# Fewer filler products, one step turned on TensorE, more masks on TensorE and another order in a fused attention and rational-MLP kernel

## The chip, the cores and the metric

One core of one Trainium2 chip. The metric is device time in microseconds (us) of one execution. Engines: PE is TensorE's products, PEld its weight loads, DVE VectorE, ACT ScalarE, POOL GpSimd (which issues most loads here), SP SyncE (which issues stores and DMA transposes).

Each run has a state: slow if it is over 1.5% above the fastest of the same kernel. Verdicts use fast runs. A ratio here is the record's, of one kernel's fast runs to the other's fast runs of the same rounds (the plain ratio of their means agrees within 0.2%). It is not quite the ratio of the medians that are quoted, which are taken over all runs. The profiled executions of both kernels were slow ones; where I compare traces I say so.

## The reference

Attention with 4 sink keys and a window of 128, batch 4, 8 heads, 768 positions, head size 64; then an MLP 512 -> 2048 -> 512 whose activation is a rational function:

```python
scores = q @ k.T / sqrt(64); keep = (pos_k < 4) | (0 <= pos_q - pos_k < 128)
x = softmax(where(keep, scores, -1e9)) @ v            # -> 3072 x 512
h = x @ w_in                                          # 3072 x 2048
P = a0 + a1*h + a2*h**2 + a3*h**3
Q = 1 + |b0|*|h| + |b1|*h**2
out = (P / (Q + 1e-6)) @ w_out
```

## The kernel before

The 3072 rows go in 12 steps of 256, three steps to a batch item. A step is attention (scores, exponentials, masks, values, normalizing), turning x, input projection (4 pieces of 16 products), elementwise work on VectorE and ScalarE, output projection (4 pieces of 8 products). All steps are cut into named pieces; one long list, ORDER, says in which order they are emitted, and each engine works through its own pieces in that order. A negative number -n in ORDER emits n filler products. The parts that the change touches:

```python
PE_MASK = (0, 1, 2, 3, 6, 9)      # steps masked by a product added to the scores
NS_PE = 2                         # steps whose k, q, x TensorE turns
...
def spin(n):                      # filler: result is never read
    for _ in range(n):
        nc.tensor.matmul(ps_scores[:, 0, 384:384 + P], lhsT=ident, rhs=ident, start=True, stop=True)

def mask(s, grp):                 # steps not in PE_MASK: VectorE multiplies the exponentials
    ...
    nc.vector.tensor_tensor(out=blocks, in0=blocks, in1=edge..., op=ALU.mult)

def turn_x(s, part):              # TensorE, through PSUM; ScalarE copies it back (place_x)
    ps = ps_hp.tile([P, 2, 512], FP32, tag="ps_h", name="ps_xT") ...
    for i in range(NPB):
        nc.tensor.transpose(ps[:, i, :], x_n[s][:, part, i * P:(i + 1) * P], ident)
def turn_x_tile(s, part):         # DMA transpose
    nc.sync.dma_start_transpose(out=x_part(s, part), in_=x_n[s][:, part, :])
...
            if s < NS_PE:
                piece(("turn_x", s, part), "PE", ...)
                piece(("placed_x", s, part), "ACT", ...)
            else:
                piece(("turn_x", s, part), "SP", ...)
...
    def parts(m):                 # elementwise work of a step in so many parts
        return 4 if m == LAST else 2 if m == 0 else 1
...
    names = list(work)
    for n in ORDER:
        if n < 0:
            spin(-n)
        elif work[names[n]].run:
            work[names[n]].run()
```

The softmax here doesn't subtract the row's maximum and nothing guards it: scores larger than these inputs give would overflow.

## Time and profile before

| | before |
|---|---|
| median (lowest to highest, 4 runs) | 272.69 us (269.80 to 273.32) |
| profiled execution, span (slow state) | 275.9 us |
| PE / DVE / ACT busy | 252.4 / 225.2 / 221.2 us |
| filler products | 372 |
| first input projection, first elementwise work | 33.3 us, 40.4 us |

The lines on which the argument rests stand in the prediction. A line of the stage view is: stretch, its length, busy time and number of instructions on PE, PEld, DVE, ACT, POOL, then granted TensorE clock, DMA share, GB/s. A line of waits is: who waited for what, total us, times, longest. A line of the chain is: start, length, what, how many.

### The profile page before, as it was taken

The page shows a single profiled execution, that of the slowest core. Times are in us where ns is not written, and L with a number is a line of the kernel's source. Part 1 is how long each engine was busy: PE and PEld are TensorE (multiplying, and loading weights), DVE is VectorE, ACT ScalarE, POOL GpSimd, SP SyncE. Part 2 cuts the span into 40 slices and gives each one's busy share as a digit, 9 for nine tenths or more (in the row PEclk, how much of TensorE's full clock was granted, in tenths as well). Part 3 has the DMA queues.
Part 4 walks back from the last instruction along what each step waited for, and adds up shares of the span by engine and source line. Part 5 has one row for each costly group of instructions (what it writes and reads, how often), then busy time and mean ns, then how long its engine had stood idle before and what let it go on. Part 6 is the DMA issues. An engine that isn't in the chain of part 4 may idle for free.

```text
span 275.9 us, 5692 instructions
## 1 busy us (share of the span) xinstructions
PE 252.4 (91%) x2344; PEld 192.4 (70%) x2344; DVE 225.2 (82%) x283; ACT 221.2 (80%) x201; POOL 118.8 (43%) x170
## 2 busy tenths in 40 slices
PE   2978898888599889999999999999999999999994
PEld 2968797777487587787776778777687776655551
DVE  3244318989917978999999999999999999999981
ACT  6084555898259669998989979999998999999870
POOL 8876677598069304083390990698000000000000
PEclk9997999999979999999999999999999999999999
DMA  6999999979999947599699999699901211211022
GB/s 140 192 162 185 117 112 129 137 85 162 118 79 90 124 74 53 130 105 180 80 74 154 124 110 203 45 139 156 122 4 39 77 57 21 76 76 40 26 88 77
DMA packets 113586, 28.72 MB, mean 104 GB/s; under 512 B 104344, under 2 KB 110488, under 8 KB 113560
## 3 DMA queue, kind: packets, MB, share of 16 engines
q0 software_dynamic: 75568, 13.00, 73.6%
q1 hardware_dynamic: 36464, 14.30, 28.8%
q10 hardware_dynamic: 1528, 1.06, 1.3%
q8 instruction: 18, 0.29, 0.5%
q14 instruction: 8, 0.07, 0.1%
HBM read 27.30 MB, written 6.29 MB: 122 GB/s over the span
## 4 chain that ended last, share of the span: by engine, by line
PE 51%; DVE 26%; ACT 12%; issue 6%; DMA 3%; POOL 1%; POOLq 0%
PE ps_out L664 19%; PE ps_h L596 16%; PE ps_s L432 5%; PE ps_o L524 4%; DMA xblk<-x_n 3%; DVE sq L634 3%; ACT lnq L640 3%; ACT e L480 3%; DVE kT L420 3%; DVE g L650 2%; PE ps_s L468 2%; DVE den L617 2%; DVE x_n L548 2%; ACT hb L603 2%; ACT den L645 2%
## 5 line engine op out<-in xcount | busy, mean ns | idle before, releaser
L596 PE MATMUL ps_h<-xblk,w_in_sb 128*128 128x256 bf16 x768 | 91.5, 276 | 2.6 <-DMA xblk<-x_n 2.5
L664 PE MATMUL ps_out<-w_out_sb,g 128*128 128x512 bf16 x368 | 86.3, 379 | 0.6 <-ACT o_t L673 0.3
L596 PEld LDWEIGHTS <-w_in_sb 128*128 128x128 bf16 x768 | 75.2, 99 | 13.5 <-issue 2.2
L238 POOL DMA_DIRECT2D v_bd<-in_v_dram x96 | 66.9, 723 | 37.1 <-PE ps_o L524 22.5
L664 PEld LDWEIGHTS <-g 128*128 128x128 bf16 x384 | 36.8, 98 | 37.2 <-issue 1.0
L603 ACT ACTIVATE hb<-ps_h 128x1024 bf16<-128x1024 f32 x48 | 48.9, 1033 | 12.9 <-PE ps_h L596 12.7
L480 ACT ACTIVATE e<-ps_s 128x768 bf16<-128x768 f32 x48 | 39.1, 816 | 11.9 <-PE ps_s L471 7.9
L640 ACT ACTIVATE lnq<-den,one_eps,qsc 128x4096 f32<-128x4096 bf16 (+2 forms) x16 | 47.2, 2956 | 0.0
L645 ACT ACTIVATE den<-lnq 128x4096 bf16<-128x4096 f32 (+2 forms) x16 | 44.1, 2771 | 0.0
L432 PE MATMUL ps_s<-ident 128*128 128x128 bf16 x372 | 28.1, 233 | 14.5 <-ACT e L480 9.3
L432 PEld LDWEIGHTS <-ident 128*128 128x128 bf16 x372 | 25.6, 106 | 16.7 <-issue 10.4
L230 POOL DMA_DIRECT2D k_bf<-in_k_dram x22 | 20.1, 916 | 35.5 <-DMA kT_flat<-k_bf 35.3
L524 PE MATMUL ps_o<-v_bd,e 128*128 128x130 bf16 x352 | 28.8, 220 | 1.2 <-DVE x_n L548 0.9
L650 DVE TENSOR_TENSOR g<-num,den 128x4096 bf16<-128x4096 bf16 (+2 forms) x16 | 28.0, 1752 | 1.6 <-ACT den L645 1.3
L468 PE MATMUL ps_s<-qT,kT 128*128 128x192 bf16 x192 | 28.1, 248 | 0.1
L621 DVE TENSOR_TENSOR den<-den,sq 128x4096 bf16<-128x4096 bf16 (+2 forms) x16 | 28.0, 1750 | 0.1
L634 DVE TENSOR_TENSOR sq<-sq,hb 128x4096 bf16<-128x4096 bf16 (+2 forms) x16 | 27.9, 1752 | 0.1
L637 DVE TENSOR_TENSOR num<-num,sq 128x4096 bf16<-128x4096 bf16 (+2 forms) x16 | 27.8, 1749 | 0.0
L524 PEld LDWEIGHTS <-e 128*128 128x128 bf16 x352 | 23.7, 97 | 5.2 <-DVE x_n L548 2.6
L610 ACT ACTIVATE sq<-hb 128x2048 bf16<-128x2048 bf16 (+1 forms) x15 | 25.4, 1695 | 0.1
L617 DVE TENSOR_SCALAR den<-hb 128x2048 uint32<-128x2048 uint32 (+2 forms) x16 | 15.9, 992 | 8.7 <-ACT hb L603 8.6
L222 POOL DMA_DIRECT2D q_bf<-in_q_dram x21 | 20.7, 996 | 0.4 <-DMA v_bd<-in_v_dram 0.4
(86 smaller groups left out, 252.4 us busy)
## 6 DMA issues: line engine op xcount, KB each, us to landing
out_dram<-o_t SPq DMA_DIRECT2D x22, 256.0 KB, 2.3
v_bd<-in_v_dram POOLq DMA_DIRECT2D x96, 32.0 KB, 4.6
k_bf<-in_k_dram POOLq DMA_DIRECT2D x22, 128.0 KB, 4.7
q_bf<-in_q_dram POOLq DMA_DIRECT2D x21, 128.0 KB, 5.2
w_in_sb<-in_moe_w_in_dram POOLq DMA_DIRECT2D x4, 512.0 KB, 7.8
w_out_sb<-in_moe_w_out_dram POOLq DMA_DIRECT2D x4, 512.0 KB, 8.1
stage_b<-in_q_dram ACTq DMA_DIRECT2D x2, 384.0 KB, 6.3
stage_a<-in_k_dram SPq DMA_DIRECT2D x2, 256.0 KB, 5.3
```

The source lines that it names most:

```text
L238: nc.gpsimd.dma_start(out=v_bd[s][e * 64:(e + 1) * 64, i, :, e, 0:D], in_=v[b, h, g * TS:(g + 1) * TS, :].rearrange("(j p) d -> p j d", p=64))
L432: nc.tensor.matmul(ps_scores[:, 0, 384:384 + P], lhsT=ident, rhs=ident, start=True, stop=True)
L468: nc.tensor.matmul(w_, lhsT=kT_fix[s % 2][:, i * NHF + n, :], rhs=qT_fix[b % 2][:, i, c:c + 192], start=True, stop=not on_pe)
L480: nc.scalar.activation(out=data.rearrange("p (a n) c -> p a n c", a=2), in_=ps[:, :, 0:384].rearrange("p a (n c) -> p a n c", n=2), func=A ...
L524: nc.tensor.matmul(ps_o[:, u, :], lhsT=l_, rhs=r_.rearrange("p e c -> p (e c)"), start=(m == 0), stop=(m == len(terms) - 1))
L596: nc.tensor.matmul(ps[:, n, :], lhsT=w_in_all[:, c, fc * P:(fc + 1) * P], rhs=xblk[m][:, c, :], start=(c == 0), stop=(c == NDMC - 1))
L603: nc.scalar.activation(out=hb[m][:, j * GW:(j + 1) * GW], in_=ps_h.pop((m, j)).rearrange("p n c -> p (n c)"), func=AF.Copy)
L634: nc.vector.tensor_tensor(out=sq[m][:, c], in0=sq[m][:, c], in1=hb[m][:, c], op=ALU.mult)
L640: nc.scalar.activation(out=lnq_fix[:, c], in_=den[m][:, c], func=AF.Ln, scale=qsc, bias=one_eps)
L645: nc.scalar.activation(out=den[m][:, c], in_=lnq_fix[:, c], func=AF.Exp, scale=-1.0)
L650: nc.vector.tensor_tensor(out=g_of[m][:, c], in0=num[m][:, c], in1=den[m][:, c], op=ALU.mult)
L664: nc.tensor.matmul(ps_out[m, tt], lhsT=g_of[m][:, co:co + P], rhs=w_out_all[:, fc, :], start=(fc == 0), stop=(fc == NFFC - 1))
```

## The change

The intent: drop nearly all fillers; spare step 2 its DMA transposes, on one of which TensorE waits; take masks off VectorE in three more steps; start step 0's elementwise work after a quarter of its projection; and lay everything out in an order made for that.

```diff
-ORDER = [ ... 968 entries, of them 27 fillers with 372 products ... ]
+ORDER = [ ... 954 entries, of them 2 fillers with 14 products ... ]
-    NS_PE = 2
+    NS_PE = 3
+    CUTS0 = (0, 1, 2, 4)
+    Q0_DVE = (2, 3)
-    PE_MASK = (0, 1, 2, 3, 6, 9)
+    PE_MASK = (0, 1, 2, 3, 5, 6, 8, 9, 10)
@@ place_q0: two of the four copies of step 0's q on VectorE
+        if i in Q0_DVE:
+            nc.vector.tensor_copy(out=dst, in_=src)
+        else:
             nc.scalar.activation(out=dst, in_=src, func=AF.Copy)
@@ the parts of a step
-    def parts(m):
-        return 4 if m == LAST else 2 if m == 0 else 1
+    def cuts(m):
+        return (0, 1, 2, 3, 4) if m == LAST else CUTS0 if m == 0 else (0, 4)
... (place_q1 for any batch item; a piece x_free; sizes from cuts)
```

## The prediction

> **What bounds the kernel now.** I read first the page of the whole span, then the chain that ended last in order of time, then the list of waits, then busy time by stage.
>
> The head of the page and its chain, by engine and line:
>
> ```profile
> span 275.9 us, 5692 instructions
> PE 252.4 (91%) x2344; PEld 192.4 (70%) x2344; DVE 225.2 (82%) x283; ACT 221.2 (80%) x201; POOL 118.8 (43%) x170
> PEclk9997999999979999999999999999999999999999
> ...
> PE ps_out L664 19%; PE ps_h L596 16%; PE ps_s L432 5%; PE ps_o L524 4%; DMA xblk<-x_n 3%; DVE sq L634 3%; ACT lnq L640 3%; ACT e L480 3%; DVE kT L420 3%; DVE g L650 2%; PE ps_s L468 2%; DVE den L617 2%; DVE x_n L548 2%; ACT hb L603 2%; ACT den L645 2%
> ```
>
> Three engines are all above 80% busy, and two things on the chain compute nothing: L432, the filler products (the order list asks for 372), with 5%, and one DMA transpose of x with 3%. Pieces of the chain in order of time (start, length, what):
>
> ```profile
> 5.16 9.08 PE ps_s L432 x113
> ...
> 33.31 1.75 PE ps_h L596 x16
> ...
> 40.42 0.83 DVE den L617
> ...
> 60.72 1.39 PE ps_s L432 x22
> ...
> 65.85 9.48 DMA xblk<-x_n
> 75.38 3.51 PE ps_h L596 x16
> ```
>
> TensorE does nothing real until 14 us; its first input projection is at 33.31, VectorE's first elementwise work at 40.42. The transpose of step 2's x takes 9.48 us, and the 16 products after it take 3.51 instead of 1.75 us, because the clock has dropped. The list of waits (total, times, longest) and the busy time by stage (PE, PE weight load, DVE, ACT, POOL):
>
> ```profile
> DVE rec L536 <- PE ps_o L524: 13.3, 9, 6.7
> ...
> PE ps_s L432 <- ACT e L480: 9.3, 9, 1.8
> ...
> DVE den L617 <- ACT hb L603: 8.6, 1, 8.6
> ```
>
> ```profile
> 33.00:42.00 9.00, 9.00 (x96) 8.23 (x95) 1.58 (x2) 5.75 (x7) 7.16 (x11) 1.00 2.09 116
> ...
> 76.00:90.00 14.00, 13.53 (x125) 10.67 (x124) 6.49 (x10) 11.09 (x7) 11.53 (x17) 0.90 1.09 86
> ...
> 105.00:255.00 150.00, 149.51 (x1271) 108.53 (x1270) 146.59 (x145) 142.50 (x115) 52.02 (x67) 1.00 0.86 95
> ```
>
> So VectorE has two holes: 8.6 us before step 0's elementwise work, and some 7.5 us at 76 to 90 (longest wait 6.7), the echo of the late x. Fillers are not free either: they write the scores' PSUM bank, so nine groups stood waiting for an exponential to empty it, and only then ran ahead of the real scores. From 105 to 255 us the three engines are 95 to 100% busy: nothing is wasted there and nothing can be won but by doing less. The loss is all ahead of 105 us, and in the end.
>
> **What the Trainium skill says.** "TensorE: Matmul & The Clock Gate", Part 1, says that the array runs at half clock until it has been busy for some 3.4 us, and falls back after about as long an idle window; a 128-column product is then 107 ns apart instead of 56. The trace agrees: 113 fillers in 9.08 us are 80 ns each, a mixture of both; and 3.51 against 1.75 us above is a factor of two after 2.5 us of idle time. This is what the fillers are for, and what their removal risks. "DMA: Bandwidth & Descriptors", Anatomy of one DMA, gives a fixed cost of about 2.0 us to a DMA; DMA Transpose (X-bar), Alternative transpose paths, names TensorE, with an identity matrix and an output in PSUM, as the other way. Here x_n's transposes land 2.4, 3.7 and 9.5 us after issue (least, median, most), so they pay the fixed cost and a queue; on TensorE four products and an ACT copy take 0.40 + 0.60 us (L571, L580).
>
> **The change, part by part.**
>
> *Fillers: 372 to 14.* Gone from the chain: L432 is 5.3% of 275.9 = 14.6 us, 9.08 of it at the start. Not all comes back, since the inputs have to arrive. In the new order the q load is issued near 3 us behind a clear; with 6.3 us to landing it is there at 9 to 10. ScalarE then has, up to x's first placing, two casts (0.84 each), four spreads (0.38), a clear (1.04), two placings of step 0's q (0.49), two of later q (0.60), five exps (0.82), two sink exps (0.28, 0.39) and one placing of x (0.60): 1.68 + 1.52 + 1.04 + 0.98 + 1.20 + 4.10 + 0.67 + 0.60 = 11.8 us. That would be 21 us without a wait; the waits at both ends (q turn, scores, attention, norm, turn), at a mostly cold clock, I put at 4 to 7.5. First input projection: 25 to 28.5, say 26.5, so 7 us earlier than 33.3.
>
> *Cold clock.* I expect a half clock for much of the first 26 us (in the waits above) and for the first 3.4 us of the projections: +1.7 us.
>
> *Step 2 turned on TensorE.* It removes the 9.48 us and the 1.75 us of cold projection, and adds on the path one turn and one placing, 1.0 us. Off the path: TensorE 8 + 8 + 8 products of 128 columns (1.4 us), ScalarE 4 placings (2.4 us). Six DMA transposes of step 2 also leave a crowded queue.
>
> *Masks of nine steps instead of six on TensorE.* Steps 5, 8, 10: VectorE loses 6 multiplications of 0.687 (4.1 us); TensorE gains 3 x 16 products of 128 columns at 56 ns (2.7 us). All in the stage where both are full, so it moves work from one co-bound to the other.
>
> *Step 0 in three parts.* The first part begins after one quarter of the projection instead of two: by one projection and its copy, some 2 us earlier. Cost: a third set of VectorE instructions (about 1 us of fixed cost) and a square of 0.7 us moved from ScalarE. Two of the four placings of step 0's q (0.49 each) move from ScalarE to VectorE, which is idle then.
>
> *Sums, three ways, in the terms of the profiled span.* Chain: 275.9 - 14.6 (fillers) - 9.5 - 1.75 + 1.0 - 2 + 4 to 5 (cold clock, later input) + 2.7 (masks, if TensorE bounds) = 256. VectorE: it starts elementwise work at 26.5 + about 3.5 (cold projection) + 1.0 (copy) = 31 instead of 40.4; it had 212 us of work from there on and 23.5 idle, tail included; now 212 - 4.1 + 2 = 210 and 23.5 less the 7.5 hole and a little = 15: 31 + 210 + 15 = 256. TensorE: real products are 768 x 0.109 + 384 x 0.216 + 432 x 0.057 + 192 x 0.082 + 96 x 0.056 + about 7.5 for sinks and turns = 220 us, now 224; about 8.5 of them fall ahead of the first projection; 26.5 + 215.5 + 1.7 (cold) + 3.9 (small waits, as now after 90 us) + 3.3 (copy and store at the end) + about 5 idle in the ramp = 256. The three agree because the engines are balanced. The profiled run was a slow one: 275.9 against a timed median of 272.47, a factor of 0.9876. 256 x 0.9876 = 253.
>
> **The rivals.** (a) *The clock.* Without fillers TensorE stays cold not only at the start but in every gap of the ramp: it did 47 us of real work before 90 us (220 less what I count after), which would double: up to 20 us lost, and the time stays near 260 to 270. For it: the factor of two is in the trace. Against: the idle gaps that fillers covered from 33 to 105 us are mostly below 2 us. (b) *Loads.* POOL issues at 0.65 to 0.9 us a piece and is busy for 25 of the first 33 us, DMA slices are at 9 up to 62 us. If everything wants its data 8 us earlier, values, keys or weights may be late: a wait on input weights or values in place of the fillers, time near 258 to 265. Against: only POOL's own instructions wait for DMA in the list, and steps 0 and 1 need no more data than before. (c) *Balance eats the gain.* Step 3's x still goes by DMA, and TensorE has some 4 us of other work between step 3's attention and its projection, less than a slow landing; a wait of 2 to 5 us there could come back: 255 to 258. (d) *The other way*: the new order also closes small waits and the ramp's idle, with 15 us of VectorE idle falling to 8: near 246.
>
> **Range and chances.** Centre 253. Low end (d), 245; high end (b) or part of (a), 262. To lose the 2% (to be above 267) nearly all of the chain's gain must be taken back by the clock or loads, which I give 5%; slower by 2%, 1%.
>
> **What would show it.** Right: first product of L596 at 25 to 29 us; L432 gone from the chain; no DMA xblk wait ahead of step 2, TensorE clock low in slices 1 to 4 and high from slice 5; VectorE's first L617 at 29 to 33 us; the longest wait of L536 below 4 us; 150 us of the middle still at 97% on DVE. Wrong: low clock digits beyond 40 us (a); waits of TensorE for w_in or v DMA, or DVE idle with POOL full (b); a DMA xblk wait above 5 us at step 3 (c); a middle that has become less dense than now, which I do not allow for at all and which would put the time above 260.

## The result, and the profile after

The changed kernel takes **261.68 us** (median of 4, 260.00 to 264.13) against 272.69: ratio 0.9596, 95% interval 0.9491 to 0.9700, so faster. It lies inside the stated range of 245 to 262, but at its upper edge and 8.7 us above the centre.

The page's head and chain of the changed kernel, and its chain in order of time:

```profile
span 262.4 us, 5089 instructions
PE 236.2 (90%) x2037; PEld 176.0 (67%) x2058; DVE 224.1 (85%) x287; ACT 222.4 (85%) x205; POOL 122.1 (47%) x170
PEclk9999999799995999999999999999999999999999
...
PE 57%; DMA 16%; DVE 11%; issue 5%; ACT 4%; POOL 4%; SPq 1%; ACTq 0%; POOLq 0%
```

```profile
42.76 3.97 DMA v_bd<-in_v_dram
46.78 1.00 PE ps_o L530 x10
47.77 3.13 PE ps_h L602 x16
...
72.48 6.12 DMA xblk<-x_n
78.65 6.57 PE ps_h L602 x32
```

Fillers are gone from the chain, and DMA has gone from 3% of it to 16%. That share is time under way, not time waited for. Two new waits of TensorE stand in the ramp, each shorter than its transfer: 3.15 us for the values of step 2 (landing at 46.7 us) and 2.58 us for the DMA transpose of step 3's x. After each one the input projection runs at half clock in this execution, a slow one: 16 products in 3.13 us, 32 in 6.57, against 1.75 per 16. The waits and stages say the same:

```profile
DVE rec L542 <- PE ps_o L530: 9.5, 11, 2.2
...
DVE den L623 <- ACT hb L609: 4.3, 2, 3.9
...
PE ps_o L530 <- DMA v_bd<-in_v_dram: 3.2, 1, 3.2
...
PE ps_h L602 <- DMA xblk<-x_n: 2.8, 2, 2.6
```

```profile
24.00:33.00 9.00, 8.86 (x96) 8.05 (x96) 4.86 (x12) 6.60 (x8) 6.91 (x10) 1.00 1.99 163
...
42.00:52.00 10.00, 6.85 (x63) 5.67 (x62) 5.10 (x10) 6.58 (x7) 9.16 (x13) 0.83 1.27 118
...
76.00:90.00 14.00, 11.37 (x78) 8.42 (x79) 8.21 (x10) 7.47 (x9) 6.72 (x8) 0.76 1.26 117
```

The start is better than predicted: the first products of L602 stand at 23.3 us in the trace (predicted 26.5), VectorE's first L623 at 26.7 (predicted 31), and that first projection runs warm. Then VectorE stands idle for 4.9 us in 42 to 52 and for 5.8 us in 76 to 90, with the clock at 0.83 and 0.76.

So two questions went to the chip. Which part brought the 11 us? And are those two holes the 9 us that are missing to 253?

### The profile page after: what moved, and what is told of

It is laid out like the page before. It is cut to its first block, busy times and chain, and to the rows that moved or that the text cites. A ratio compares the mean times of both kernels' runs of the same rounds, so it can differ in the third digit from the quotient of the medians.

```text
span 262.4 us, 5089 instructions
## 1 busy us (share of the span) xinstructions
PE 236.2 (90%) x2037; PEld 176.0 (67%) x2058; DVE 224.1 (85%) x287; ACT 222.4 (85%) x205; POOL 122.1 (47%) x170
## 4 chain that ended last, share of the span: by engine, by line
PE 57%; DMA 16%; DVE 11%; issue 5%; ACT 4%; POOL 4%; SPq 1%; ACTq 0%; POOLq 0%
PE ps_out L670 22%; PE ps_h L602 22%; PE ps_o L530 7%; DMA v_bd<-in_v_dram 6%; DMA w_out_sb<-in_moe_w_out_dram 3%; PE ps_s L474 3%; DMA xblk<-x_n 2%; DMA q_bf<-in_q_dram 2%; DMA out_dram<-o_t 2%; DVE sq L640 2%; DVE den L627 2%; POOL v_bd L240 2%; ACT lnq L646 1%; DVE x_n L554 1%; PE ps_s L670 1%
## 5 line engine op out<-in xcount | busy, mean ns | idle before, releaser
L602 PE MATMUL ps_h<-xblk,w_in_sb 128*128 128x256 bf16 x768 | 95.3, 280 | 3.0 <-DMA xblk<-x_n 2.8
L670 PE MATMUL ps_out<-w_out_sb,g 128*128 128x512 bf16 x348 | 83.9, 379 | 4.2 <-ACT o_t L679 3.1
L602 PEld LDWEIGHTS <-w_in_sb 128*128 128x128 bf16 x768 | 76.0, 101 | 16.2 <-DMA xblk<-x_n 2.8
L474 PE MATMUL ps_s<-qT,kT 128*128 128x192 bf16 x192 | 30.0, 248 | 1.6 <-ACT e L486 0.9
L232 POOL DMA_DIRECT2D k_bf<-in_k_dram x22 | 22.8, 1037 | 16.9 <-issue 8.4
L530 PEld LDWEIGHTS <-e 128*128 128x128 bf16 x352 | 24.3, 97 | 8.5 <-issue 4.1
L616 ACT ACTIVATE sq<-hb 128x2048 bf16<-128x2048 bf16 (+1 forms) x15 | 24.4, 1626 | 0.1
L477 PE MATMUL ps_s<-nege,ident 128*128 128x128 bf16 x144 | 23.2, 222 | 0.0
L474 PEld LDWEIGHTS <-kT 128*128 128x128 bf16 x192 | 18.5, 98 | 4.0 <-issue 1.0
L623 DVE TENSOR_SCALAR den<-hb 128x2048 uint32<-128x2048 uint32 (+2 forms) x17 | 16.3, 961 | 4.3 <-ACT hb L609 4.3
```

The source lines that it names most:

```text
L474: nc.tensor.matmul(w_, lhsT=kT_fix[s % 2][:, i * NHF + n, :], rhs=qT_fix[b % 2][:, i, c:c + 192], start=True, stop=not on_pe)
L530: nc.tensor.matmul(ps_o[:, u, :], lhsT=l_, rhs=r_.rearrange("p e c -> p (e c)"), start=(m == 0), stop=(m == len(terms) - 1))
L602: nc.tensor.matmul(ps[:, n, :], lhsT=w_in_all[:, c, fc * P:(fc + 1) * P], rhs=xblk[m][:, c, :], start=(c == 0), stop=(c == NDMC - 1))
L670: nc.tensor.matmul(ps_out[m, tt], lhsT=g_of[m][:, co:co + P], rhs=w_out_all[:, fc, :], start=(fc == 0), stop=(fc == NFFC - 1))
```

## The experiments

All twelve kernels gave the right result. Names with b_ start from the kernel before, with a_ from the changed one. My theory 1: fillers and waits lengthen the chain, each gives back about its share, and in the changed kernel the two new holes take part of it again. The rival, theory 2: fillers pay for themselves by the clock, and the new order makes the gain.

| run | median us (lowest to highest, runs) | ratio to before, 95% |
|---|---|---|
| b_nofill | 263.73 (261.93 to 265.61, 4) | 0.971 (0.958 to 0.984) |
| b_nofill_start | 269.34 (268.11 to 270.47, 4) | 0.989 (0.978 to 1.000) |
| b_x2_pe | 270.81 (269.58 to 273.35, 20) | 0.997 (0.994 to 1.000) |
| b_mask9 | 275.24 (272.92 to 282.47, 16) | 1.010 (1.007 to 1.014) |
| b_parts | 265.89 (264.02 to 267.26, 6) | 0.979 (0.973 to 0.984) |
| changed kernel | 261.68 (260.00 to 264.13, 4) | 0.960 (0.949 to 0.970) |
| a_x2_dma | 266.43 (261.74 to 269.80, 4) | none given |
| a_cuts2 | 261.44 (259.63 to 264.49, 6) | 0.962 (0.956 to 0.968) |
| a_mask6 | 274.47 (272.35 to 277.79, 16) | 1.007 (1.003 to 1.010) |
| a_v2_first | 261.52 (258.77 to 266.26, 6) | 0.955 (0.948 to 0.961) |
| a_x3_pe | 259.63 (258.58 to 260.44, 6) | 0.952 (0.948 to 0.957) |
| a_v2_x3 | 257.18 (255.15 to 260.01, 6) | 0.941 (0.934 to 0.948) |
| a_v2_x3_o3 | 256.82 (253.31 to 260.22, 6) | 0.942 (0.934 to 0.950) |

The kernel before, run beside them, had medians of 272.6 to 273.5 us. At the 2% line the record calls the changed kernel, a_v2_first, a_x3_pe and a_v2_x3 faster, b_x2_pe, b_mask9 and a_mask6 the same, and the rest unclear (a_x2_dma has no verdict).

### b_nofill: only the fillers go

```diff
     names = list(work)
-    for n in ORDER:
+    for n in [n for n in ORDER if n >= 0]:
```

> The kernel before with all 372 filler products left out and nothing else changed. Theory 1 (fillers only lengthen the chain, 14.6 us of it, of which the start gives back some 6): 259 to 266 us. Theory 2 (they keep the clock up and are worth their time): within 2% of before or slower, 268 to 280 us, with several low digits in the clock row between 35 and 100 us. In either the first projection should come at 25 to 28 us instead of 33.

Measured: 263.73 us, ratio 0.971, some 8 us of the 11. All four runs lie in the range of theory 1 and none in that of theory 2, and the low clock digits of theory 2 are missing but for one. (That the gain is above 2% is likely and not certain: the interval reaches 0.984.) The clock row of this run, its largest wait of TensorE, and the ramp:

```profile
PEclk9999999979999999999999999999999999999999
```

```profile
PE ps_t L391 <- DMA q_bf<-in_q_dram: 9.3, 1, 9.3
```

```profile
42.00:66.00 24.00, 20.39 (x205) 17.54 (x203) 22.05 (x27) 20.41 (x22) 17.83 (x24) 0.93 1.30 124
```

One digit of the clock row is low, and the clock from 42 to 66 us is 0.93 on average instead of 1.00. From about 17 us on the array stays warm on the real work alone, but for that one digit. Before that it is cold, though the row shows 9: eight turns of k take 0.85 us from 15.94 us on, against 0.49 us for the same eight at 13.39 us in the changed kernel. The first group of 113 had mostly covered a wait for q, which now shows as 9.3 us; what it cost beyond that is the few us by which the trace's first projection moved, from 30.4 us (in the profile of b_x2_pe, which starts as before does) or 33.1 us (in that of before) to 26.8 us. The two traces of the same start differ by 2.7 us; half of this is that the same 113 products took 7.78 us in b_x2_pe's fast execution and 9.08 in the slow one of before, where the clock from 14 to 24 us was also 0.84 instead of 1.00.

### b_nofill_start: only the fillers ahead of the first projection

```diff
+    first = ORDER.index(names.index(("gemm1", 0, 0)))
+    for n in [n for at, n in enumerate(ORDER) if n >= 0 or at > first]:
```

> The kernel before without the fillers ahead of the first input projection only; those of the ramp stay. If the start is what counts (theory 1) it gains 5 to 8 us, 264 to 268, and the ramp's fillers explain the rest of b_nofill. If a start that is 7 us earlier is used up by later waits for loads or for step 2's x, under 3 us: 269 to 273.

Measured: 269.34 us, ratio 0.989 (0.978 to 1.000). That is about 3 us, below the 5 to 8 of theory 1 and at the edge of the rival's range. The first projection stands at 27.6 us in this fast trace against 30.4 us in the fast one of b_x2_pe, which has the old start: 2.8 us, so an earlier start was passed on whole, and it was only smaller than expected. All four runs of b_nofill lie below all four of this one. So the start gives some 3 us and the ramp's fillers the larger rest, some 5 of the 8. In the ramp fillers stand in front of scores and wait for the bank that the exponential still reads (9.3 us in 9 waits in the kernel before).

### b_x2_pe: only step 2's x on TensorE

```diff
-            if s < NS_PE:
+            if s < 3:                      # turn_x, placed_x only
+    for p_ in (1, 0):                      # the copy right behind its turn
+        ORDER.remove(names.index(("placed_x", 2, p_)))
+        ORDER.insert(1 + ORDER.index(names.index(("turn_x", 2, p_))), names.index(("placed_x", 2, p_)))
```

> The kernel before with step 2's x turned on TensorE and placed by ScalarE instead of the DMA transpose that the chain waits 9.48 us for. Theory 1: the 9.5 us and the cold projection of 1.75 us go and 1 to 3 us come instead, 263 to 266 us. Rival: something just behind (ScalarE, w_out or step 3's loads) takes its place and it gains under 4 us.

A miss. 20 runs: ratio 0.997, interval 0.9935 to 1.0003, so below 2 us, where the chain had promised 8 to 10. The list of waits of the kernel before shows why: of the 9.48 us that the transpose was under way, TensorE stood still for 2.5, because it had other work beside it.

```profile
PE ps_h L596 <- DMA xblk<-x_n: 2.5, 1, 2.5
```

And this profile is of a slow execution. A fast one with the same transpose and the same order from the first projection on is that of b_nofill_start. Its chain has:

```profile
59.69 7.74 DMA xblk<-x_n
67.47 1.92 PE ps_h L596 x16
```

TensorE waits 0.7 us there, and the projection behind is not cold (1.92 us for 16 products, where the prediction has 3.51). The hole of VectorE that follows, in before, in b_nofill_start and in this run:

```profile
83.44 0.18 DVE L536 RECIPROCAL rec<-ps_o 128x4 f32<-128x4 f32 x1 [6.73 <-PE ps_o L524]
```

```profile
73.87 0.18 DVE L536 RECIPROCAL rec<-ps_o 128x4 f32<-128x4 f32 x1 [2.88 <-PE ps_o L524]
```

```profile
75.88 0.18 DVE L536 RECIPROCAL rec<-ps_o 128x4 f32<-128x4 f32 x1 [2.55 <-PE ps_o L524]
```

So a hole of 6.73 us belongs to the slow execution; of the fast one's 2.88 us the move to TensorE takes away 0.3. From the first projection to step 2's projection it takes 39.8 us with the DMA transpose (b_nofill_start) and 39.1 us without (this run): 0.7 us, the size of the 0.3%. In a fast execution hardly anything was there to win.

### a_x2_dma: the same part undone in the changed kernel

```diff
                 free = [("x_free", s)] if free else []
+            if s < 2:
                 piece(("turn_x", s, part), "PE", ...)
```

> The changed kernel with step 2's x turned by DMA again, the rest (k and q of step 2 on TensorE, few fillers, order) as changed. If turning x on TensorE is worth its chain share, 267 to 271 us. If the later waits (values of step 2, x of step 3) bound the ramp anyway, 261 to 264 us.

Four runs from 261.74 to 269.80, median 266.43, and no ratio was given, since only one of them counts as fast. That one, 261.74, is the changed kernel's time; the other three (266.4 to 269.8) are slow ones, and so is the profile, in which the projection waits 6.6 us for the transpose of x. By the fast run this part is worth nothing in the new order, but one run settles no size. Whether the DMA transpose makes slow executions more frequent or longer is left open too.

### a_mask6: masks of steps 5, 8 and 10 back on VectorE

```diff
-    PE_MASK = (0, 1, 2, 3, 5, 6, 8, 9, 10)
+    PE_MASK = (0, 1, 2, 3, 6, 9)
```

> The changed kernel with the masks of steps 5, 8 and 10 back on VectorE (six multiplications of 0.69 us), TensorE rid of 48 products of 128 columns (2.7 us). If VectorE bounds the middle: 2 to 4 us slower, 264 to 266. If TensorE bounds it: 1 to 3 us faster. If both hold each other: within 1 us.

A miss of all three forecasts: 274.47 us, 12.8 us slower than the changed kernel and slower than before. It is not busy time (the six masks are 4.1 us of VectorE); it is waiting. TensorE waits 11.6 us in all for normalizations of attention, against 1.0 us in the changed kernel, which by size is most of the 12.8. The line of waits, and the timeline around the longest:

```profile
PE ps_o L530 <- DVE x_n L554: 11.6, 7, 7.3
```

```profile
147.88 0.69 DVE L493 TENSOR_TENSOR e<-e,edge 128x1024 bf16<-128x1024 bf16 x1 [3.14 <-ACT e L486]
151.29 0.69 DVE L493 TENSOR_TENSOR e<-e,edge 128x1024 bf16<-128x1024 bf16 x1 [2.72 <-ACT e L486]
...
163.71 0.19 DVE L542 RECIPROCAL rec<-ps_o 128x6 f32<-128x6 f32 x1
...
164.61 0.61 PE L530 MATMUL ps_o<-v_bd,e 128*128 128x130 bf16 x4 [7.30 <-DVE x_n L554]
```

The mask instruction is short, but VectorE takes its instructions in order: it stands 3.14 and 2.72 us in front of the two masks until ScalarE has done the exponentials. After that come seven elementwise instructions (151.9 to 163.7 us) that lay ahead of the normalization in the list; so the normalization is at 163.7, and TensorE, whose next attention group needs the bank that it frees, waits 7.30 us. The order was made for a kernel without these masks, so this is not what they cost in an order of their own.

### b_mask9: the same masks onto TensorE in the kernel before

```diff
-    PE_MASK = (0, 1, 2, 3, 6, 9)
+    PE_MASK = (0, 1, 2, 3, 5, 6, 8, 9, 10)
```

> The kernel before with the masks of steps 5, 8 and 10 on TensorE as well, nothing else. By busy time VectorE sheds 4.1 us and TensorE, as full, gains 2.7 us: within 1 us of before, 271 to 274. If what counts is the wait of VectorE's queue for the exponentials in front of each mask (a_mask6 was 13 us slower than the changed kernel, by which it would be a main part of the gain): 3 to 6 us faster, 266 to 269.

Neither forecast: 1.0% slower (1.007 to 1.014), which on 272.6 us is 2.8 us (1.9 to 3.7). The 48 added products are 2.7 us of TensorE. VectorE's relief of 4.1 us shows nowhere in the time, and the loss has the size of what TensorE takes on. That agrees with TensorE being the bound of the old order there, though no run isolates it further.

### b_parts: no fillers, x of step 2 and nine masks on TensorE, the old order

The edits of b_nofill, b_x2_pe and b_mask9 together.

> The kernel before without its fillers, with step 2's x on TensorE and with nine masks on TensorE, but in its own order: what the parts give without the new order. If the parts carry the gain: 258 to 262 us, as the changed kernel. If the new order carries a good share: 264 to 268.

265.89 us, ratio 0.979, between the two forecasts. It is also what the three parts give one by one: -7.9 (b_nofill), -0.8 (b_x2_pe) and +2.8 us (b_mask9) make -5.9, and 0.979 is -5.9 us. So 4 us by the medians and 5 by the ratios lie between it and the changed kernel (intervals 0.973 to 0.984 and 0.949 to 0.970, which do not meet): the new order, with what was not brought over (k and q of step 2, three parts, q copies on VectorE), gives these. Against b_nofill the two added parts gained nothing (0.979 against 0.971, intervals overlapping).

### a_cuts2: step 0 in two halves

```diff
-    CUTS0 = (0, 1, 2, 4)
+    CUTS0 = (0, 2, 4)
+    at = names.index(("and", 0, 0))        # the first part's ten entries go, the halves take the others' places
+    seq = [n if n < at else n - 10 for n in ORDER if not at <= n < at + 10]
```

> The changed kernel with step 0's elementwise work in two halves instead of a quarter, a quarter and a half; the halves stand where the second and third parts stood. VectorE then starts it one projection and one copy later (2 to 3 us), with ten instructions fewer (1 us). If the early start is worth what the prediction said: 1 to 3 us slower, 263 to 265. If the holes at 42 and 76 us swallow it: within 1 us.

261.44 us against 261.68: the rival's within 1 us. VectorE's first L623 is at 29.8 us in this trace instead of 26.7, and nothing comes of it at the end. The trace is of a fast execution and has both holes, smaller: TensorE waits 2.38 us for the values, with full clock behind, and 2.31 us for step 3's x, with 32 products in 4.99 instead of 3.66 us behind.

### a_v2_first: the values of step 2 earlier

```diff
+    late = [names.index(nm) for nm in [("load_w_out", 1)] + [("load_vss", h) for h in (4, 6, 5, 2, 1)]]
+    seq = [n for n in ORDER if n not in late]
+    at = 1 + max(seq.index(names.index(("load_v", 2, h))) for h in range(H))
+    seq[at:at] = late
```

> The changed kernel with one load of output weights (512 KB) and five small loads of sink values moved on GpSimd from among step 2's value loads to behind them. Theory: the hole at 42 to 52 us is a late load (3.15 us of TensorE waiting for v, then a cold projection of 3.13 instead of 1.75 us), so TensorE's wait for v_bd goes below 1 us, and the time falls by 1 to 4 us, to 258 to 261. Rival: the ramp is bound by what follows (step 3's x), the hole moves, under 1 us gained.

By the median nothing: 261.52. The profiled execution was a slow one (266.26), 4.6 us above the changed kernel's median, so what follows may be of that execution. Its waits and stages:

```profile
PE ps_out L670 <- DMA w_out_sb<-in_moe_w_out_dram: 3.3, 2, 3.0
```

```profile
42.00:52.00 10.00, 9.83 (x122) 9.06 (x121) 9.55 (x18) 9.85 (x12) 5.76 (x9) 1.00 2.16 88
52.00:66.00 14.00, 10.72 (x69) 6.84 (x68) 8.61 (x8) 8.19 (x10) 11.59 (x14) 0.76 1.40 152
```

The hole at 42 to 52 is filled. But the output weights, which I had put behind the values, are now what TensorE waits for, with the clock down again: in this execution the hole moved to 52 to 66. In the fast profile of a_v2_x3 below, which has the same loads, that wait is 1.0 us.

### a_x3_pe: step 3's x on TensorE too

```diff
-            else:
+            elif s == 3:                   # as for s < NS_PE
+                piece(("turn_x", s, part), "PE", ...); piece(("placed_x", s, part), "ACT", ...)
+            else:
                 piece(("turn_x", s, part), "SP", ...)
+    x3 = [names.index((nm, 3, p_)) for p_ in (1, 0) for nm in ("turn_x", "placed_x")]
+    seq = [n for n in ORDER if n not in x3]
+    at = 1 + seq.index(names.index(("gemm2", 0, 1, 1)))
+    seq[at:at] = x3
```

> The changed kernel with step 3's x turned on TensorE too, behind the second output product of step 0. Theory: the hole at 76 to 90 us is the DMA transpose of step 3's x (2.6 us of waiting, then 32 cold products in 6.57 instead of 3.5 us, 4.2 us of ScalarE and 5.5 us of VectorE waiting), so no xblk wait before 90 us and 3 to 6 us gained, 256 to 259. Rival: the time stands at 260 to 263, because v loads or GpSimd then end the wait.

259.63 us: 2 us below the changed kernel by the medians, less than the 3 to 6 expected, and the intervals of the ratios overlap. The hole at 76 to 90 us is gone from its trace (VectorE 12.77 of 14 us busy there, clock 1.00), the one at 42 to 52 stays.

### a_v2_x3: both

The two edits together.

> Both of the last two together. If the miss of the prediction (9 us) lies in these two holes: 252 to 257 us. If they share one cause behind them (loads as a whole being late), no better than the better of the two alone.

**257.18 us**, ratio 0.941 (0.934 to 0.948), whose interval lies wholly below that of the changed kernel. It beats both kernels, and it is the upper end of what was expected (252 to 257). From its profile, a fast execution with a span of 254.3 us:

```profile
42.00:52.00 10.00, 9.83 (x124) 9.09 (x122) 9.54 (x19) 9.84 (x11) 6.47 (x10) 1.00 1.56 146
52.00:66.00 14.00, 12.98 (x121) 10.21 (x119) 12.46 (x11) 13.69 (x13) 11.66 (x15) 1.00 1.47 146
66.00:76.00 10.00, 7.56 (x68) 5.18 (x66) 8.39 (x11) 8.37 (x8) 6.24 (x9) 1.00 1.54 146
76.00:90.00 14.00, 14.00 (x137) 11.03 (x135) 13.49 (x16) 12.62 (x14) 12.00 (x15) 1.00 1.17 93
```

Both holes are filled and the clock is at 1.00 in these stages. 3.1 us of VectorE's idle time and 3.5 us of TensorE's turn up again between 52 and 76 us.

### a_v2_x3_o3: three output buffers

```diff
-    o_sb = ctx.enter_context(tc.tile_pool(name="o_sb", bufs=2))
+    o_sb = ctx.enter_context(tc.tile_pool(name="o_sb", bufs=3))
```

> a_v2_x3 (values of step 2 ahead, step 3's x on TensorE) with three output buffers instead of two, for the ScalarE wait of 2.9 us for a store in the changed kernel at 149 us. If that wait costs in the end: 253 to 256 us against 257.2. If it was chance, or hidden: within 1 us of 257.2.

256.82 us, the same. The 2.9 us that ScalarE waited for a store at 149 us in the changed kernel's slow trace cost nothing that these runs can tell; in the trace of a_v2_x3, which is what this run changes, the wait is 1.4 us.

## Why the prediction was right or wrong

**Faster, and inside the range: right, with the main reason right.** Fillers were called a cost and not a help. b_nofill shows it: without them the time falls by 2.9%, and the clock stays up. Rival (a) is refuted for the old order. In the new one its sign, low digits beyond 40 us, did come, but behind waits for data.

**Fillers at the start: the bound was named, the share was not.** The prediction had the inputs arriving late and so a gain of 7 us at the start. Removing the fillers of the start alone (b_nofill_start) moves the first projection by 2.8 us in fast traces and the time by 3 us. In the changed kernel it comes 10 us earlier than in before (both slow traces); what of this the new order brings is not isolated. Most of the fillers' price lay in the ramp, which the prediction named (nine groups waiting for a bank) and did not price by itself.

**Cold clock: the place was wrong.** Predicted was a half clock for much of the first 26 us and +1.7 us at the first projection. There the products ran warm from about 13 us on; the cold ones came behind the two later waits, with 3.13 - 1.75 = 1.4 us and 6.57 - 3.50 = 3.1 us in the slow profile. The fast one of a_cuts2 has 1.3 us, behind the second wait only.

**Step 2 on TensorE, "it removes the 9.48 us and the 1.75 us": the term that failed.** In the old order it is worth under 2 us. The time that a DMA was under way was read as time that TensorE would save. TensorE stood still for 2.5 us of it, which the list of waits said; in a fast execution with the same transpose (b_nofill_start) for 0.7 us, with no cold projection behind.

**VectorE's sum, "23.5 less the 7.5 hole and a little = 15": the term that was mis-sized.** The prediction set 31 + 210 + 15 = 256 for a slow profile. Measured: start at 26.7, 210.4 us busy from there on (224.1 less 13.7 ahead of it), so 262.4 - 26.7 - 210.4 = 25.3 us idle. The start was 4.3 us better and the idle time 10.3 us worse: together the 6 us between 256 and 262.4. And 4.9 + 5.8 = 10.7 us of that idle time lie in the two stretches with the new waits; the other 14.6 us are the predicted 15. The two waits were rivals (b), late loads, and (c), step 3's x by DMA. Each was named; neither was in the sum, and both came true. a_v2_x3 shows that they cost 4.5 us by the medians (1.9% by the ratios), half of the 8.7 that were missing. Another 2.3 us are the conversion at the end: the factor 0.9876 was taken from a profile well above its median, while in the changed kernel the median over the profiled span is 261.68 / 262.4 = 0.997. What is left is not settled by a run: as these two holes close, 3 us of new idle time appear on each of two engines right behind.

**Masks: the busy times were right, the reading was not.** "It moves work from one co-bound to the other" left out that a mask on VectorE is also a wait in VectorE's queue. In the old order the move cost 2.8 us, the size of TensorE's 2.7; in the new order taking it back cost 12.8.

**Three parts: wrong by its 2 us.** a_cuts2 shows no difference. That VectorE's earlier start ends in the hole at 42 us is likely and not shown.

**The new order** was given nothing of its own in the sum, except as rival (d). b_parts puts it and the smaller parts at 4 to 5 us. So the number owes something to luck: the chain's sum had 10 us for step 2's x, which measured under 2, and nothing for the order, which gave back half of that error.

**The middle stays dense: nearly right.** VectorE is busy 130.2 of 135 us from 105 to 240 us, 96%, against 131.8 (98%) before.

## What to carry to other kernels

Price a DMA on the chain by how long an engine stands still for it, not by how long it is under way, and look at a fast execution before you do: here 9.5 us under way were 2.5 us of waiting in a slow profile and 0.7 us in a fast one, and removing them brought under 2 us. When a start moves forward by 10 us, go through every load and DMA transpose that had slack before: here two of them became the new waits, and in the slow profile each cost its wait and a stretch of cold clock. In kernels laid out as fixed queues a short instruction that waits is dear not by its own length, but by all that stands behind it, so test a part and its order together.

## What the Trainium skill lacked or had wrong

- "TensorE: Matmul & The Clock Gate", Part 1, advises to avoid idle gaps of over some 3.4 us. Here shorter recorded gaps were followed by half clock: 2.58 us ahead of the 32 products in 6.57 us, after a stretch of thin work (three groups of scores, the sinks and one output product piece in the 7 us before), and 2.49 us in the kernel before. A gap of 2.38 us in a_cuts2 was followed by full clock. So the length of one gap does not decide; what does is not shown, and the page has no number for short gaps that follow one another.
- The same page says how long the warm-up lasts, but no page has the price of filler products that keep the clock up. Here 372 of them cost 2.9% (b_nofill), and real work kept the clock at 0.88 or more in each stage after the start without them. That the warm-up's length varies between runs, as the page says, agrees: the same 113 products took 7.78 and 9.08 us.
- "DMA: Bandwidth & Descriptors", Anatomy of one DMA, gives its fixed cost of about 2.0 us for the DMAs that GpSimd issues. The transposes of x are issued by SyncE, and no page has the time from issue to landing of such a one beside busy loads ("VectorE: DVE Perf Modes", The three transpose paths, times a 128x128 one and says nothing of loads). These SBUF-to-SBUF transposes of x landed 2.4 (least), 2.8 (median) and 6.2 us (most) after issue in the changed kernel, 2.4, 3.7 and 9.5 before; the most lay 3.8 and 7.1 us above the least.
- The first page says in Part 1 (Architectural detail) that VectorE and ScalarE are strict first-in, first-out. The runs agree and add a size that no page gives: with six masks of 0.69 us put back into VectorE's queue, two of them behind waits of 3.14 and 2.72 us, the whole kernel was 12.8 us slower (a_mask6).
